# Weight conversions move their exponent word from SBUF to a PSUM bank, and GpSimd waits for earlier VectorE port work

## The chip, the cores and the metric

One core of one Trainium2 chip runs the whole program in one launch. The metric is device time in microseconds; lower is better. Engines are named as the profile names them: PE (TensorE matmul), DVE (VectorE), ACT (ScalarE), POOL (GpSimd), SP (SyncE, which issues most DMAs).

## The reference, cut to what matters

```
# 1. filter by FFT:   Y = rfft(x, axis=1) * (filt_r + 1j*filt_i);  y = irfft(Y)     x: 8 x 3072 x 256
# 2. top-1 experts over the 24576 rows of y: 8 experts, at most 768 tokens each
logits = x @ w_gate; e = argmax(logits); gate_w = softmax(logits)[e]
h = maximum(disp[e] @ w1[e], 0);  y = h @ w2[e]        # 256 -> 1024 -> 256; dropped tokens give 0
out[i] = gate_w[i] * y[...]
# 3. dense block on every row; w_in and w_out come as float64
h = x @ w_in                                            # 256 -> 2048
g = maximum(h, 0) + log1p(exp(-abs(h)))
return (g @ w_out).astype(float32)                      # 2048 -> 256
```

## The kernel before, in words

Tokens fill the experts in order, so the kernel filters the first three of the eight batches statically (STATIC = 3), and filters more only if a flag at the end says that an expert still has room. The expert part runs in 16 units of 384 tokens (UNIT), an expert and one half of its capacity each. Every float32 product is split into a high and a low part, so each matmul is done three times (high by high, high by low, low by high). The splits are made by ACT, which rounds to the high part (names in h: w1h, hh, gh, yh), and by POOL or DVE, which subtract to get the low part (w1l, w2l, gl on POOL; hl, yl, xl on DVE).

A unit transposes its tokens (pt), multiplies by w1 (pw, then hh and hl), by w2 (py, then yh and yl), by w_in (pi, then softplus in ACT's ab, ab, ln and DVE's g, then gh and gl) and by w_out (po). w_in and w_out are float64 in memory, and there are 16 conversions of 128x512 pieces: for each, `split_res` reads the two 32-bit words of a number. DVE first masks the mantissa into a scratch word v, combines it with the low word into wf, then overwrites v with the exponent field (three instructions); ACT scales the exponent word; DVE adds the sign to v and multiplies wf by it (two instructions); ACT and POOL split wf. In the planner these parts are the nodes ("c", n, 0) to ("c", n, 4). The scratch v is named pv where it lies in PSUM and wv where it lies in SBUF. Conversions 0 to 5 borrow v from the PSUM pool psy (3 banks, tag y), 6 to 8 from pso (2 banks), and 9 to 15 have it in SBUF (TURN = (6, 9)). psa is a third PSUM pool, of 3 banks.

Each batch also makes a table that sorts tokens to expert slots. The gate's DVE steps (nodes ("g", b, 4) and on; oh at L473, ctot at L496) and the one-hot tiles lo and hv (L512, eight pairs in each batch) belong to it; POOL multiplies hv by the token number, PE sums the table, DVE adds it up (ts).

The first part, about 310 us long, mixes all this: the three batches, the conversions and units 0 to 3. Its order is found by `Plan` as the program is built. Each piece of work is a node with an engine, a cost in ns, nodes that it comes after, and buffers of rings that it takes and gives (BUFS). A greedy list scheduler keeps a clock for each engine and picks the node that can start first; of equals the one whose chain of successors is longest, to which the table LIFT adds. Nodes with lock=True on DVE or POOL also share one clock named port: of those the scheduler lets one run at a time. The resulting list is written out in order, so every engine gets its instructions in the list's order and waits in it only for data and buffers. The scheduler's clock itself waits for nothing on the chip: nothing keeps a DVE and a POOL node with lock=True apart when the program runs. From step 16 on (STEPS), units follow in a fixed order by steps, in which each of the three products of a unit has its turn; there a unit's py takes two of psy's three banks.

Of the kernel before, what the change touches and what calls it, by code (L numbers as in the profile page):

```python
# [24 lines left out]
UNIT = 384  # L25
# [70 lines left out]
class Plan:  # L96
# [2 lines left out]

    BUFS = {"a": 3, "y": 3, "o": 2, "it": 4, "z": 3, "t2": 2, "j": 4, "yt": 3, "xt": 8, "s1": 3, "e0": 1, "e1": 1,  # L100
            "gx": 1, "gsb": 1, "lo": 2, "wst": 3, "wf": 2, "ws": 5, "w1h": 3, "w2h": 3, "xd": 3, "x": 2, "h": 4, "Y": 3,
            "wv": 1, "ln": 3, "g": 3, "gg": 4}
    LIFT = {"c_12": 45110, "c_15": 107406, "gl_0": 14316, "hh_3": 46195, "keep": 221952, "park_2": 380830,
            "t_0": 212010761652706638821731995831060079811112206336, "t_1": 416284, "t_2": 112004,
            "w2_1": 54516, "w2_2": 36883, "wi_0": 39454, "wo_0": 6694, "xh_3": 73006, "xl_1": 157432,
            "yh_0": 152114}
    MID = 4000
    HOP = {"PE": 250, "ACT": 130, "DVE": 130, "POOL": 100, "SP": 0}

# [92 lines left out]
def body(tc, cap, x, ff, fx, wg, w1, w2, win, wout, m1, m2, m3, m4, small, out):  # L202
# [14 lines left out]
    idxd = dram.tile([2, 128, nblk], I32, name="idxd")  # L217
    mid = [dram.tile([N1 * N2, D], F32, name=f"mid{b}") for b in range(1, STATIC)]
    psa = ctx.enter_context(tc.tile_pool(name="psa", bufs=3, space=PSUM))
    psy = ctx.enter_context(tc.tile_pool(name="psy", bufs=3, space=PSUM))  # L220
    pso = ctx.enter_context(tc.tile_pool(name="pso", bufs=2, space=PSUM))

    sm = const.tile([128, small.shape[1]], F32, name="sm")
    ident = sm[:, 0:128]
# [16 lines left out]
    ebias = const.tile([128, 1], F32, name="ebias")  # L241
    nc.vector.memset(ebias, -8.0 * 0x38000000)


    class Conv:

# [92 lines left out]
        def s2(self, b, kk):  # L339


            its = [self.it.pop((b, 2 * kk + f)) for f in range(2)]
            ps = [psy.tile([128, 2, D], F32, name="p3", tag="y") for _ in range(2)]
            for f in range(2):
                for c in range(4):
                    for a in range(2):
                        rows = slice(64 * a, 64 * a + 64)
                        nc.tensor.matmul(ps[a][32 * c:32 * c + 32, f],
                                         lhsT=self.m2s[rows, 4 * kk + 2 * f + c % 2, 32 * (c // 2):32 * (c // 2) + 32],
                                         rhs=its[f][rows, c % 2], start=True, stop=True)  # L350
            self.ps["s2", b, 2 * kk], self.ps["s2", b, 2 * kk + 1] = ps
# [206 lines left out]
        nc.vector.scalar_tensor_tensor(out=si, in0=slot, scalar=-1.0, in1=free, op0=ALU.add, op1=ALU.add)  # L558
        return gi, si

    class P:
        pass

    def wi_pools(st, tag):
        pool = lambda n, b: st.enter_context(tc.tile_pool(name=tag + n, bufs=b, side="right", reuse_waits="tile"))
        wp = pool("wi", 1)
# [33 lines left out]
    def split_res(q, which, space):  # L600
# [10 lines left out]
        if f64:  # L611
            two = t.bitcast(U32).rearrange("p (f two) -> p f two", two=2)
            lw, hw = two[:, :, 0], two[:, :, 1]
            if space is None:
                v = P.wl.tile([128, 512], U32, name="wv", tag="wv", bufs=1)
            else:
                v = space.tile([128, 512], U32, name="pv", tag="y" if space is psy else "o")
            f = P.wl.tile([128, 512], F32, name="wf", tag="wf")
            nc.vector.tensor_scalar(v, hw, 0xFFFFF, 0x100000, op0=ALU.bitwise_and, op1=ALU.bitwise_or)  # L619
            nc.vector.scalar_tensor_tensor(out=f, in0=lw, scalar=2.0 ** -32, in1=v, op0=ALU.mult, op1=ALU.add)  # L620
            nc.vector.tensor_scalar(v, hw, 0x7FF00000, None, op0=ALU.bitwise_and)  # L621
            yield 0
# [33 lines left out]
    class Unit:  # L656
# [211 lines left out]
    with tc.manual_schedule():  # L868
# [182 lines left out]
        def make_room():  # L1051
            stf.close()
            right_pools(stw, "M")

        def low_room():
            ste.close()
            low_pool(stw, "M")
# [27 lines left out]
            q = i % 4  # L1085
            return max(16 * (v - 2) + 4 * q - (8 if i < 4 else 6), -7 if i < 4 else -4)

        STEPS, HEAD, TURN = 16, 4, (6, 9)
        early = [(v, i) for v in range(2) for q in range(4) for i in (q, q + 4)] + [(2, i) for i in (0, 4, 1, 5)]
        pieces = early + [p[1:] for p in sorted((split_at(v, i), v, i) for v in range(2, len(units)) for i in range(8)  # L1090
                                                if (v, i) not in early)]
# [12 lines left out]
        for v in range(HEAD):  # L1104
# [12 lines left out]
            for j in range(8):  # L1117
# [7 lines left out]
                add(("hl", v, j), "DVE", 557, lambda u=u, j=j: u.w1_l(j), after=[("hh", v, j)], give=[("a", n)])  # L1125
                if v < 2 or 16 * (v - 2) + 2 * j < STEPS:
                    add(("w2", v, j), "PE", 1044, lambda u=u, j=j: u.w2_p(j),
                        after=[("hl", v, j), ("wl", v, 4 + j // 2)] + [],
                        behind=[("w2", v, j - 1)] if j else [("w2", v - 1, 7)] if v else [],
                        take=["y", "y"] if j == 0 else [],  # L1130
                        give=[("h", ("hh", v, j)), ("w2h", ("wh", v, 4 + j // 2))], tail=2000)
            for d in range(2 if ("w2", v, 7) in plan.node else 0):
                add(("yh", v, d), "ACT", 490, lambda u=u, d=d: u.y_h(d), after=[("w2", v, 7), "low"],
                    take=["Y"] if d == 0 else [], behind=[("yh", v, 0)] if d else [])
                add(("yl", v, d), "DVE", 550, lambda u=u, d=d: u.y_l(d), after=[("yh", v, d)],
                    give=[("y", ("w2", v, 0))])


        spaces, turn = [psy, pso, None], ["y", "o", "wv"]
        res = [(q, which) for which in range(2) for q in range(KI // 2)]  # L1140
        for n, (q, which) in enumerate(res):
            kind = (n >= TURN[0]) + (n >= TURN[1])
            load(("r", n), lambda q=q, which=which: load_res(q, which), 512, after=["x_done"], take=["wst"], behind=[("r", n - 1)] if n else [])
            stage = lambda: step_of(conv, n, lambda q=q, which=which, kind=kind: split_res(q, which, spaces[kind]))
            room = ["x_done", ("tf", last, 11)] if n < WI0 else ["room"] if n < KI // 2 else ["left"]
            add(("c", n, 0), "DVE", 1560 if kind == 2 else 2070, stage(), after=[("r", n), *room], take=[turn[kind], "wf"],
                behind=[("c", n - 1, 2)] if n else [], lock=kind == 2)
            add(("c", n, 1), "ACT", 663, stage(), after=[("c", n, 0)])
            add(("c", n, 2), "DVE", 1375, stage(), after=[("c", n, 1)], give=[(turn[kind], ("c", n, 0)), ("wst", ("r", n))])
# [7 lines left out]
        for v, u in enumerate(units):  # L1157
            for i in range(KI):
# [10 lines left out]
                if t + 4 < STEPS:  # L1169
# [2 lines left out]
                        behind=prior("wo", v, i - 1) if i else [("s4", last, 15), ("g", last, 10), "flags"] +  # L1172
                        [("c", n, 2) for n in range(*TURN)])

        order = plan.order(plan.LIFT)
        assert len(order) == len(plan.node)
        for n in order:
            plan.node[n][2]()


        at = {}
# [199 lines left out]
```

## Time and profile before

| | us |
|---|---|
| median of 3 runs | 1074.15 (1073.12 to 1076.38) |
| profiled execution, its own time | 1073.57 |
| its span, first to last instruction | 1071.7 |
| PE busy | 1029.2 |
| DVE, ACT, POOL busy | 495.9, 778.7, 600.5 |

The span is what the profile shows; the profiled execution's own time is 1.9 us more, which lies around it. Busy times are averages over two very different parts, the planned one up to about 310 us and the steps behind it, so the rows below take them apart by stretches of time.

### The profile page before, as it was taken

How to read it: one execution, taken by the hardware profiler on the slowest of the kernel's cores; microseconds unless marked ns; L12 is line 12 of the kernel's file. 1: busy time of each engine (PE TensorE's matmuls, PEld its weight loads, DVE VectorE, ACT ScalarE, POOL GpSimd, SP SyncE). 2: the span in 40 equal slices, each digit the busy share in tenths (PEclk: the TensorE clock that was granted, in tenths of full speed). 3: DMA queues.
4: the chain of work that ended last, by engine and by line, in shares of the span. 5: the costliest groups of instructions: out<-in, count | busy, mean ns of one | idle time of the engine just before them, and what ended most of it. 6: DMA issues, size and time to landing. Idle time of an engine off the chain costs nothing.

```text
span 1071.7 us, 19029 instructions
## 1 busy us (share of the span) xinstructions
PE 1029.2 (96%) x7112; PEld 954.9 (89%) x7112; DVE 495.9 (46%) x887; ACT 778.7 (73%) x1612; POOL 600.5 (56%) x560
## 2 busy tenths in 40 slices
PE   8999999898899999999999999999999999999994
PEld 7655666697899999999999999999999999999994
DVE  3856799899877433233323233333333233333221
ACT  4565568666677777777778777787877787878882
POOL 0513445587575556866666665657575747554553
PEclk9999999999899999999999999999999999999997
DMA  9978638553111453333332332322121212100000
GB/s 283 292 231 238 204 93 275 185 184 116 55 35 40 172 197 133 124 114 124 106 121 95 113 116 105 133 91 69 40 70 48 72 41 69 31 16 1 16 16 18
DMA packets 72822, 120.03 MB, mean 112 GB/s; under 512 B 6928, under 2 KB 46736, under 8 KB 72720
## 3 DMA queue, kind: packets, MB, share of 16 engines
q1 hardware_dynamic: 65424, 96.69, 28.1%
q0 software_dynamic: 4608, 12.59, 3.4%
q10 hardware_dynamic: 2688, 9.44, 2.7%
q8 instruction: 58, 0.95, 0.4%
q14 instruction: 44, 0.36, 0.1%
HBM read 71.51 MB, written 47.19 MB: 111 GB/s over the span
## 4 chain that ended last, share of the span: by engine, by line
PE 67%; DVE 4%; issue 2%; POOL 1%; ACT 1%; DMA 0%; POOLq 0%; DVEq 0%; ACTq 0%
PE po L816 23%; PE pi L784 23%; PE pw L730 10%; PE py L759 10%; POOL gl L801 1%; DVE wf L620 1%; PE pt L707 1%; DVE g L650 1%; DVE wv L619 0%; DVE wv L621 0%; DVE wf L627 0%; DVE hl L742 0%; DVE wv L625 0%; DMA out_dram<-ot,si 0%; ACT ab L643 0%
## 5 line engine op out<-in xcount | busy, mean ns | idle before, releaser
L650 DVE SCALAR_TENSOR_TENSOR g<-pi,ln 128x384 f32<-128x384 f32 x256 | 142.3, 556 | 478.6 <-ACT ln L645 418.6
L801 POOL TENSOR_TENSOR gl<-g,gh 128x384 fp32r<-128x384 f32 x256 | 260.4, 1022 | 125.7 <-ACT gh L796 122.0
L816 PE MATMUL po<-woh,gh 128*128 128x256 f32 x768 | 216.3, 282 | 3.8 <-DVE ot L823 3.8
L816 PE MATMUL po<-woh,gl 128*128 128x256 f32 x768 | 216.1, 281 | 0.0
L816 PE MATMUL po<-wol,gh 128*128 128x256 f32 x768 | 215.9, 281 | 0.0
L642 ACT ACTIVATE ab<-pi 128x384 f32<-128x384 f32 x256 | 124.5, 486 | 122.2 <-PE pi L784 116.0
L784 PE MATMUL pi<-yh,wih 128*128 128x384 f32 x512 | 173.2, 338 | 2.0 <-DVE g L650 2.0
L784 PE MATMUL pi<-yh,wil 128*128 128x384 f32 x512 | 173.5, 339 | 0.0
L784 PE MATMUL pi<-yl,wih 128*128 128x384 f32 x512 | 173.3, 338 | 0.0
L682 POOL TENSOR_TENSOR w1l<-ws,w1h 128x512 fp32r<-128x512 f32 x64 | 83.5, 1305 | 119.3 <-ACT w1h L677 91.8
L816 PEld LDWEIGHTS po<-woh,gh 128*128 128x128 f32 x768 | 144.0, 188 | 6.3 <-ACT ab L642 2.5
L816 PEld LDWEIGHTS po<-wol,gh 128*128 128x128 f32 x768 | 145.0, 189 | 0.0
L816 PEld LDWEIGHTS po<-woh,gl 128*128 128x128 f32 x768 | 144.7, 188 | 0.0
L645 ACT ACTIVATE ln<-ab 128x384 f32<-128x384 f32 (+1 forms) x257 | 134.9, 525 | 8.1
L643 ACT ACTIVATE ab<-ab 128x384 f32<-128x384 f32 (+1 forms) x257 | 134.8, 525 | 8.1
L796 ACT CAST gh<-g 128x384 fp32r<-128x384 f32 x256 | 129.8, 508 | 4.3 <-DVE g L650 3.6
L682 POOL TENSOR_TENSOR w2l<-ws,w2h 128x512 fp32r<-128x512 f32 x64 | 84.2, 1316 | 54.8 <-ACT w2h L677 54.8
L784 PEld LDWEIGHTS pi<-yh,wih 128*128 128x128 f32 x512 | 96.5, 188 | 2.6 <-DVE g L650 2.6
L784 PEld LDWEIGHTS pi<-yl,wih 128*128 128x128 f32 x512 | 96.5, 188 | 0.0
L784 PEld LDWEIGHTS pi<-yh,wil 128*128 128x128 f32 x512 | 96.4, 188 | 0.0
L730 PE MATMUL pw<-xh,w1h 128*128 128x384 f32 x256 | 88.3, 345 | 6.2 <-DVE g L650 3.4
L368 POOL TENSOR_TENSOR z<-z,t 128x512 f32<-128x512 f32 x36 | 46.5, 1293 | 77.6 <-DVE t L363 72.1
(146 smaller groups left out, 1932.3 us busy)
## 6 DMA issues: line engine op xcount, KB each, us to landing
ws<-in_w_dram SPq DMA_DIRECT2D x128, 256.0 KB, 2.9
out_dram<-cs SPq DMA_DIRECT2D x48, 512.0 KB, 4.0
xt<-in_x_dram SPq DMA_DIRECT2D x24, 384.0 KB, 7.5
mid<-s ACTq DMA_DIRECT2D x16, 384.0 KB, 4.5
rowsd<-yt SPq DMA_DIRECT2D x16, 384.0 KB, 3.7
it<-mid SPq DMA_DIRECT2D x24, 256.0 KB, 4.2
wst<-in_win_dram SPq DMA_DIRECT2D x8, 512.0 KB, 5.3
wst<-in_wout_dram SPq DMA_DIRECT2D x8, 512.0 KB, 3.7
```

Of the source, the lines that this page charges most:

```text
L368: nc.gpsimd.tensor_tensor(out=z, in0=z, in1=t2, op=ALU.add)
L642: nc.scalar.activation(out=ab[:, :n], in_=h, func=ACTF.Abs)
L643: nc.scalar.activation(out=ab[:, :n], in_=ab[:, :n], func=ACTF.Exp, scale=-1.0)
L645: nc.scalar.activation(out=ln[:, :n], in_=ab[:, :n], func=ACTF.Ln, bias=1.0)
L650: nc.vector.scalar_tensor_tensor(out=g[:, :n], in0=h, scalar=0.0, in1=ln[:, :n], op0=ALU.max, op1=ALU.add)
L682: nc.gpsimd.tensor_tensor(out=lo, in0=self.ws.pop(i), in1=hi.bitcast(F32), op=ALU.subtract)
L730: nc.tensor.matmul(ps, lhsT=a[:, k, fs], rhs=b[:, k], start=(n == 0), stop=(n == 5))
L759: nc.tensor.matmul(self.py[d], lhsT=a[:, j % 2, ds], rhs=b, start=(j == 0 and n == 0), stop=(j == 7 and n == 2))
L784: nc.tensor.matmul(pi, lhsT=a[i // 2][:, i % 2, k], rhs=b[:, k], start=(n == 0), stop=(n == 5))
L796: nc.scalar.copy(gh, self.g[i])
L801: nc.gpsimd.tensor_tensor(out=gl, in0=g, in1=gh.bitcast(F32), op=ALU.subtract)
L816: nc.tensor.matmul(self.po[t], lhsT=a[:, ts], rhs=b[:, i], skip_group_check=True, start=(i == 0 and n == 0 and t != 1), stop=(i == KI - 1 ...
```

## The change

It has four parts. **The bank.** The pools psa (3 banks) and pso (2) stay; psy is opened as P.py and lives until a node "turn", which closes it and opens two pools in its three banks: psw with 2 banks for py (ring yy) and psv with 1 bank for v (ring v). All of the conversions 6 to 15 take v from that bank; in the planner they are no longer lock=True. py is made in psw from the first unit on, so its first tile stands behind "turn". **The wait.** When the list is written out, the last instruction of each DVE node with lock=True is remembered, and the first instruction of every POOL node with lock=True that follows in the list gets a semaphore wait for it. There is no such wait the other way. **The order.** LIFT has other numbers, and with the other rings they give another list in the planned part. **The steps.** Their order stays; py alternates between two banks where it had three.

```diff
-            "wv": 1, "ln": 3, "g": 3, "gg": 4}
-    LIFT = {"c_12": 45110, "c_15": 107406, "gl_0": 14316, "hh_3": 46195, "keep": 221952, "park_2": 380830,
...
+            "yy": 2, "v": 1, "ln": 3, "g": 3, "gg": 4}
+    LIFT = {"c_10": 12614.0, "c_15": -10845.0, "hl_0": 91105.0, "hl_3": 34417.0, "keep": 221107.0,
...
-    psy = ctx.enter_context(tc.tile_pool(name="psy", bufs=3, space=PSUM))
     pso = ctx.enter_context(tc.tile_pool(name="pso", bufs=2, space=PSUM))
+    ctx.push(lambda *_: P.close.close())
...
+    def wide(name):
+        P.close = ExitStack()
+        P.py = P.close.enter_context(tc.tile_pool(name=name, bufs=3, space=PSUM))
+
+    wide("psy")
...
-                v = space.tile([128, 512], U32, name="pv", tag="y" if space is psy else "o")
+                pool, tag = space()
+                v = pool.tile([128, 512], U32, name="pv", tag=tag)
...
+        def turn():
+            P.close.close()
+            P.close = ExitStack()
+            P.py = P.close.enter_context(tc.tile_pool(name="psw", bufs=2, space=PSUM, reuse_waits="tile"))
+            P.pv = P.close.enter_context(tc.tile_pool(name="psv", bufs=1, space=PSUM, reuse_waits="tile"))
...
-        STEPS, HEAD, TURN = 16, 4, (6, 9)
+        STEPS, HEAD, TURN = 16, 4, (6, 6)
...
-                        after=[("hl", v, j), ("wl", v, 4 + j // 2)] + [],
+                        after=[("hl", v, j), ("wl", v, 4 + j // 2), "turn"],
...
-                        take=["y", "y"] if j == 0 else [],
+                        take=["yy", "yy"] if j == 0 else [],
...
-        spaces, turn = [psy, pso, None], ["y", "o", "wv"]
+        spaces = [lambda: (P.py, "y"), lambda: (pso, "o"), lambda: (P.pv, "v")]
+        add("turn", "SP", 0, turn, after=[("tf", last, k) for k in range(12)] + [("c", n, 2) for n in range(TURN[0])])
...
-            add(("c", n, 0), "DVE", 1560 if kind == 2 else 2070, stage(), after=[("r", n), *room], take=[turn[kind], "wf"],
-                behind=[("c", n - 1, 2)] if n else [], lock=kind == 2)
+            add(("c", n, 0), "DVE", 2070, stage(), after=[("r", n), *room] + ["turn"] * (kind > 1), take=[tag, "wf"],
+                behind=[("c", n - 1, 2)] if n else [])
...
+        lanes = {"DVE": mybir.EngineType.DVE, "POOL": mybir.EngineType.Pool}
         order = plan.order(plan.LIFT)
         assert len(order) == len(plan.node)
+        held = None
         for n in order:
+            here = len(nc.cur_bb.bb.instructions)
             plan.node[n][2]()
+            if plan.node[n][7] and len(nc.cur_bb.bb.instructions) > here:
+                new = [i for i in nc.cur_bb.bb.instructions[here:] if i.engine == lanes[plan.node[n][0]]]
+                if plan.node[n][0] == "DVE":
+                    held = new[-1]
+                elif held is not None:
+                    tc.add_manual_dep(new[0], held.name, mybir.DependencyInfo(
+                        mybir.DependencyClass.Sync, mybir.DependencyReason.DATA), reason="shared port")
```

The line numbers of the changed kernel are 7 to 27 higher; L512 of before is L521 there, L619 is L626, and so on.

Three places show what the change does to an engine's row. First DVE late in the planned part, before: the end of one conversion and the start of the next, with the scratch word in SBUF (wv), and the next softplus sum g behind them.

```order
L625 SCALAR_TENSOR_TENSOR wv<-wst,wv 128x512
L627 SCALAR_TENSOR_TENSOR wf<-wf,wv 128x512
L619 TENSOR_SCALAR wv<-wst 128x512
L620 SCALAR_TENSOR_TENSOR wf<-wst,wv 128x512
L621 TENSOR_SCALAR wv<-wst 128x512
L650 SCALAR_TENSOR_TENSOR g<-pi,ln 128x384
L742 SCALAR_TENSOR_TENSOR hl<-pw,hh 128x384
L512 TENSOR_TENSOR lo_82<-sm,ij_81 96x512
```

The same engine in the changed kernel, at the corresponding place.

```order
L632 SCALAR_TENSOR_TENSOR pv<-wst,pv 128x512
L634 SCALAR_TENSOR_TENSOR wf<-wf,pv 128x512
L626 TENSOR_SCALAR pv<-wst 128x512
L627 SCALAR_TENSOR_TENSOR wf<-wst,pv 128x512
L628 TENSOR_SCALAR pv<-wst 128x512
L541 TENSOR_TENSOR ts<-ts,p_3064 128x48
L776 TENSOR_TENSOR yl<-py,yh 128x384
L521 TENSOR_TENSOR lo_81<-sm,ij_78 96x512
```

The five instructions of a conversion are the same in number and kind; their scratch operand is now in PSUM.

Second, the last gate step of batch 2 (ctot to ij) on DVE before: it stands behind both halves of conversion 7 and most of the first products of units 0 and 1.

```order
L625 SCALAR_TENSOR_TENSOR pv<-wst,pv 128x512
L627 SCALAR_TENSOR_TENSOR wf<-wf,pv 128x512
L742 SCALAR_TENSOR_TENSOR hl<-pw,hh 128x384
L496 TENSOR_TENSOR ctot<-ctot,cn 96x8
L497 TENSOR_TENSOR eo<-eo,ixf 96x32
```

In the changed kernel it stands between the two halves of conversion 6.

```order
L628 TENSOR_SCALAR pv<-wst 128x512
L749 SCALAR_TENSOR_TENSOR hl<-pw,hh 128x384
L723 TENSOR_TENSOR xl<-pt,xh 128x384
L505 TENSOR_TENSOR ctot<-ctot,cn 96x8
L506 TENSOR_TENSOR eo<-eo,ixf 96x32
```

So the table of batch 2 can start earlier, ahead of conversion 7.

Third, POOL, with the semaphores that each instruction waits for, before: the low parts of conversions 1 and 2 (wil) and the gathers of unit 0's tokens (xd).

```order
L519 TENSOR_TENSOR hv_85<-hv_85,sm 96x192 [waits DVE_49,PE_49]
L638 TENSOR_TENSOR wil_1362<-wf,wih_1358 128x512 [waits Activation_49]
L638 TENSOR_TENSOR wil_1363<-wf,wih_1359 128x512 [waits Activation_49]
L697 DMA xd<-rowsd,gi_2361 128x256 [waits DMAHW2_49,DMAHW3_49,DMAHW1_49,DMAHW4_49,DMAHW0_49,DVE_49]
L697 DMA xd<-rowsd,gi_2361 128x256 x2
```

The same in the changed kernel.

```order
L528 TENSOR_TENSOR hv_82<-hv_82,sm 96x192 [waits PE_49]
L645 TENSOR_TENSOR wil_1314<-wf,wih_1310 128x512 [waits DVE_49,Activation_49]
L645 TENSOR_TENSOR wil_1315<-wf,wih_1311 128x512 [waits DVE_49,Activation_49]
L704 DMA xd<-rowsd,gi_2361 128x256 [waits DMAHW2_49,DMAHW3_49,DMAHW1_49,DMAHW4_49,DMAHW0_49,DVE_49]
L704 DMA xd<-rowsd,gi_2361 128x256 x2
```

Both wil now also wait for DVE: the first for the gate's oh of batch 2, the second for the end of batch 1's table.

## Rows read from the trace of the kernel before

**Rows 1.** Page, part 1: busy us of each engine (share, instructions).
```profile
PE 1029.2 (96%) x7112; PEld 954.9 (89%) x7112; DVE 495.9 (46%) x887; ACT 778.7 (73%) x1612; POOL 600.5 (56%) x560
```

**Rows 2.** Windows: stretch, length, busy us by engine, granted clock, DMA share, GB/s.
```profile
180.00:204.00 24.00, 20.68 (x101) 12.52 (x100) 20.94 (x45) 18.26 (x42) 11.08 (x12) 1.00 0.73 234
224.00:254.00 30.00, 23.36 (x132) 22.08 (x132) 27.38 (x46) 16.90 (x35) 22.31 (x20) 0.94 0.47 148
...
278.00:310.00 32.00, 27.15 (x172) 26.34 (x171) 28.45 (x41) 21.29 (x45) 18.23 (x17) 0.89 0.11 35
310.00:1000.00 690.00, 686.23 (x4556) 682.77 (x4556) 233.52 (x424) 535.34 (x1123) 423.17 (x396) 1.00 0.26 89
```

**Rows 3.** Waits of PE from 180 to 312 us: total us, times, longest.
```profile
PE pw L730 <- DVE g L650: 3.4, 1, 3.4
PE pt L707 <- DVE ts L532: 2.4, 1, 2.4
PE pw L730 <- DVE hl L742: 2.2, 1, 2.2
PE p L428 <- DVE j L393: 1.9, 1, 1.9
PE pt L707 <- DMA xd<-rowsd,gi: 1.9, 3, 0.8
```

**Rows 4.** Windows, instructions on the SBUF word wv alone: busy us (count).
```profile
150.00:312.00 162.00, 34.31 (x35) 5.05 (x7) 0.97 0.45 143
```

**Rows 5.** Windows, instructions on the PSUM word pv alone, same stretch.
```profile
150.00:312.00 162.00, 30.87 (x45) 5.96 (x9) 0.97 0.45 143
```

**Rows 6.** Groups by line and shape on DVE: xcount | busy us, mean ns.
```profile
L619 DVE TENSOR_SCALAR pv<-wst 128x512 uint32<-128x512 uint32 x9 | 6.2, 684 | 0.0
L619 DVE TENSOR_SCALAR wv<-wst 128x512 uint32<-128x512 uint32 x7 | 6.0, 864 | 0.0
...
L473 DVE TENSOR_TENSOR oh<-v,vm 96x256 f32<-96x256 f32 x3 | 4.4, 1480 | 0.0
...
L496 DVE TENSOR_TENSOR ctot<-ctot,cn 96x8 f32<-96x8 f32 x3 | 2.8, 928 | 0.0
```

**Rows 7.** Timeline of DVE: start us, duration us.
```profile
186.26 3.23 DVE L473 TENSOR_TENSOR oh<-v,vm 96x256 f32<-96x256 f32 x1
...
220.76 2.47 DVE L496 TENSOR_TENSOR ctot<-ctot,cn 96x8 f32<-96x8 f32 x1
...
243.92 6.03 DVE L512 TENSOR_TENSOR lo<-sm,ij 96x512 fp32r<-96x512 f32 x1
```

**Rows 8.** Tile lo from 180 to 312 us: duration ns min/median/max.
```profile
L512 DVE TENSOR_TENSOR lo<-sm,ij x10: 674/901/6034, 182.2 to 297.4; 96x512 fp32r<-96x512 f32 x10
```

**Rows 9.** Windows, DVE instructions on tile lo alone.
```profile
180.00:312.00 132.00, 16.40 (x10) 0.96 0.40 129
```

**Rows 10.** Timeline of POOL: start us, duration us.
```profile
186.54 2.49 POOL L638 TENSOR_TENSOR wil<-wf,wih 128x512 fp32r<-128x512 f32 x2
...
221.90 1.30 POOL L682 TENSOR_TENSOR w1l<-ws,w1h 128x512 fp32r<-128x512 f32 x1
...
243.50 1.28 POOL L682 TENSOR_TENSOR w1l<-ws,w1h 128x512 fp32r<-128x512 f32 x1
...
248.42 0.98 POOL L801 TENSOR_TENSOR gl<-g,gh 128x384 fp32r<-128x384 f32 x1
```

**Rows 11.** Timeline of PE at the two clocks: start us, duration us.
```profile
282.98 0.52 PE L730 MATMUL pw<-xl,w1h 128*128 128x384 f32 x1
...
289.56 0.34 PE L730 MATMUL pw<-xl,w1h 128*128 128x384 f32 x1
```

**Rows 12.** Timeline of DVE in the first batch: a table waits for PE.
```profile
72.27 0.69 DVE L512 TENSOR_TENSOR lo<-sm,ij 96x512 fp32r<-96x512 f32 x1 [2.41 <-PE p L527]
```

**Rows 13.** Timeline of the later stage: end of one unit, start of the next.
```profile
617.80 1.08 DVE L769 TENSOR_TENSOR yl<-py,yh 128x384 fp32r<-128x384 f32 x2
...
622.92 0.33 PE L759 MATMUL py<-hh,w2h 128*128 128x384 f32 x1
```

More of the change, by code (lines that the diff above doesn't have):

```diff
@@ L101 @@
             "gx": 1, "gsb": 1, "lo": 2, "wst": 3, "wf": 2, "ws": 5, "w1h": 3, "w2h": 3, "xd": 3, "x": 2, "h": 4, "Y": 3,
-            "wv": 1, "ln": 3, "g": 3, "gg": 4}
-    LIFT = {"c_12": 45110, "c_15": 107406, "gl_0": 14316, "hh_3": 46195, "keep": 221952, "park_2": 380830,
-            "t_0": 212010761652706638821731995831060079811112206336, "t_1": 416284, "t_2": 112004,
-            "w2_1": 54516, "w2_2": 36883, "wi_0": 39454, "wo_0": 6694, "xh_3": 73006, "xl_1": 157432,
-            "yh_0": 152114}
+            "yy": 2, "v": 1, "ln": 3, "g": 3, "gg": 4}
+    LIFT = {"c_10": 12614.0, "c_15": -10845.0, "hl_0": 91105.0, "hl_3": 34417.0, "keep": 221107.0,
+            "park_2": 374450.0, "su_0": 25618.0, "t_0": 5.2642809135285573e+51, "t_1": 406929.0,
+            "t_2": 44830.0, "turn": 125636.0, "xh_1": 100850.0, "xl_2": 103004.0, "yh_1": 27623.0,
+            "yl_2": 5645.0}
     MID = 4000
@@ L242, in body @@
     nc.vector.memset(ebias, -8.0 * 0x38000000)
+    class P:
+        pass
+    def wide(name):
+        P.close = ExitStack()
+        P.py = P.close.enter_context(tc.tile_pool(name=name, bufs=3, space=PSUM))
+    wide("psy")
     class Conv:
@@ L342, in s2 @@
             its = [self.it.pop((b, 2 * kk + f)) for f in range(2)]
-            ps = [psy.tile([128, 2, D], F32, name="p3", tag="y") for _ in range(2)]
+            ps = [P.py.tile([128, 2, D], F32, name="p3", tag="y") for _ in range(2)]
             for f in range(2):
@@ L559, in slot_index @@
         return gi, si
-    class P:
-        pass
     def wi_pools(st, tag):
@@ L752, in w2_p @@
             if j == 0:
-                self.py = [psy.tile([128, UNIT], F32, name="py", tag="y") for _ in range(2)]
+                self.py = [P.py.tile([128, UNIT], F32, name="py", tag="y") for _ in range(2)]
             hi, lo = self.wv[4 + j // 2]
@@ L1135, in body @@
                 add(("yl", v, d), "DVE", 550, lambda u=u, d=d: u.y_l(d), after=[("yh", v, d)],
-                    give=[("y", ("w2", v, 0))])
-        spaces, turn = [psy, pso, None], ["y", "o", "wv"]
+                    give=[("yy", ("w2", v, 0))])
+        spaces = [lambda: (P.py, "y"), lambda: (pso, "o"), lambda: (P.pv, "v")]
+        add("turn", "SP", 0, turn, after=[("tf", last, k) for k in range(12)] + [("c", n, 2) for n in range(TURN[0])])
         res = [(q, which) for which in range(2) for q in range(KI // 2)]
@@ L1142, in body @@
             kind = (n >= TURN[0]) + (n >= TURN[1])
+            tag = "yov"[kind]
             load(("r", n), lambda q=q, which=which: load_res(q, which), 512, after=["x_done"], take=["wst"], behind=[("r", n - 1)] if n else [])
@@ L1145, in body @@
             room = ["x_done", ("tf", last, 11)] if n < WI0 else ["room"] if n < KI // 2 else ["left"]
-            add(("c", n, 0), "DVE", 1560 if kind == 2 else 2070, stage(), after=[("r", n), *room], take=[turn[kind], "wf"],
-                behind=[("c", n - 1, 2)] if n else [], lock=kind == 2)
+            add(("c", n, 0), "DVE", 2070, stage(), after=[("r", n), *room] + ["turn"] * (kind > 1), take=[tag, "wf"],
+                behind=[("c", n - 1, 2)] if n else [])
             add(("c", n, 1), "ACT", 663, stage(), after=[("c", n, 0)])
-            add(("c", n, 2), "DVE", 1375, stage(), after=[("c", n, 1)], give=[(turn[kind], ("c", n, 0)), ("wst", ("r", n))])
+            add(("c", n, 2), "DVE", 1375, stage(), after=[("c", n, 1)], give=[(tag, ("c", n, 0)), ("wst", ("r", n))])
             add(("c", n, 3), "ACT", 615, stage(), after=[("c", n, 2)])
@@ L1233, in body @@
         stw.close()
+        P.close.close()
+        wide("psg")
     fv = nc.values_load(flag[0:1, 0:1], min_val=0, max_val=1)
```

## Prediction

> **What bounds the kernel now.** I read the page first. PE is busy in 96% of the span [rows 1], so only three things can make the kernel faster: less idle time on PE, fewer microseconds at a low clock, or a shorter tail. The windows say where they are [rows 2]. From 310 to 1000 us PE is busy for 686.23 of 690 us at full clock; nothing is to be had there. From 180 to 310 us it is different. In three stretches PE idles 24 - 20.68 = 3.3, 30 - 23.36 = 6.6 and 32 - 27.15 = 4.9 us, 14.8 in all, and two of them have a mean granted clock under 1 (0.94 and 0.89). The two levels are seen in single matmuls: the same one takes 0.52 us just after a long wait and 0.34 soon after [rows 11], which is 1.2 against 2.4 GHz. The loss in busy time is (1 - 0.94) x 23.36 = 1.4 and (1 - 0.89) x 27.15 = 3.0 us, 4.4 in all.
>
> Next, who is waited for. The longest waits of PE there all name DVE: for g 3.4, for ts 2.4, for hl 2.2, for j 1.9 us; the gathers (DMA xd) account for 1.9 [rows 3]. DVE is busy 20.94 of 24, 27.38 of 30 and 28.45 of 32 us in these stretches, more than any other engine but PE [rows 2]. So the planned part is bound by DVE in places, and what DVE does in vain there PE pays for. Of the 14.8 us of idle I take off the gathers' 1.9, which the change doesn't touch: 12.9 us of idle and 4.4 of low clock, **17.3 us, are what DVE's lateness costs**.
>
> Last, why DVE is late. Its instructions are stretched. The 35 on wv take 34.31 us, 4.90 for each of seven conversions [rows 4]; the 45 on pv take 30.87 us, 3.43 for each of nine [rows 5]. The difference, 1.47 x 7 = **10.3 us**, is time lost in conversions 9 to 15. The table's lo has a least duration of 674 ns and a greatest of 6034 [rows 8]; ten of them take 16.40 us [rows 9], 16.40 - 10 x 0.67 = 9.7 too much. The gate's oh at 186.26 takes 3.23 us [rows 7], where the three have 4.4 in all [rows 6], so that the other two have 0.59 each: 2.6 too much. ctot at 220.76 takes 2.47 of its group's 2.8, so 0.17 is its usual time: 2.3 too much. These locked nodes together lose **14.6 us**. What they stand against is seen in POOL: during lo's 6.03 us from 243.92 POOL runs one piece after another, from 243.50 to 249.40, five instructions in a row [rows 7, 10].
>
> **The change part by part.** *The bank.* Seven conversions (9 to 15) go from 4.90 to 3.43 us on DVE: 10.3 us less. I take the mean of pv, whose instructions keep one duration. Conversions 6 to 8 only change banks: nothing. Bounds: below, nothing gained, if pv beside POOL's denser work were stretched like wv; above, the 10.3.
>
> The SBUF form has one advantage: an undisturbed mask into wv is short. Its group's mean is 864 ns with the disturbed ones in it, against 684 for pv [rows 6], so the trace's mean speaks for PSUM. The Trainium skill (VectorE: DVE Perf Modes, "Why PSUM operands drop a tier") says that a PSUM operand keeps a float32 copy or scalar operation out of its faster two-port mode, which speaks against this change. By the page alone (an estimate: a mask at half of 684 ns before, so 14 x 0.34 = 4.8 us more) the bank would be a loss of 4.8 us on DVE; by the trace, whose sums contain both effects, it is a gain of 10.3. The same skill (SBUF — State Buffer, "Who interferes with whom") says that an instruction with at most one SBUF input outside that mode doesn't meet GpSimd, which would explain pv's constant duration; the trace agrees with 684 and 864 ns.
>
> *The wait.* It holds back only POOL work that stands behind the DVE node in the list. At oh both wil (2.49 us from 186.54 [rows 10]) would wait: the hv ahead of them ends at about 186.6, so oh would end at 187.2 instead of 189.5, 2.3 us earlier. At ctot only the w1l at 221.90 stands behind it: 1.3 of the 2.3. At the long lo four of the five POOL pieces stand ahead of it, and only the gl at 248.42 (0.98) would wait: 1.0 of 5.4. That is 4.6 of 10.3, 45%. The other lo's I take alike: of 14.6 us the wait removes 6.6 and leaves **8.0**, if POOL runs as late against DVE as now. Bounds: 0 and 14.6.
>
> What the wait costs: queued behind it in POOL's order are wil, w1l, w2l and gl, for which PE's conversions, first and second products and the output product wait. Behind the gate and table of batch 2 there are some 16 such waits. Each can hold POOL for the DVE node's own time, 0.67 us for a lo [rows 8], so at most 11 us. But POOL is idle 12.9, 7.7 and 13.8 us in the three stretches [rows 2], and among the long waits of PE [rows 3] none is for w1l, w2l or gl. I take nothing and keep the 11 us for a rival.
>
> *The later py and the two banks.* The first py stands behind "turn", so behind conversion 5; five first products stand ahead of it instead of three, so PE has work meanwhile. In the steps, a unit's last yl ends at 617.80 + 1.08 = 618.88, and the next unit's first py begins at 622.92 [rows 13]; two banks must be free there, and 4.0 us cover it. I take nothing. Without that cover each of 13 later units would lose what yl is late.
>
> *The order.* PE issues the same matmuls, the queues the same DMAs. The last gate step of batch 2 moves ahead of conversion 7, which lets its table begin earlier; I give it no time of its own, and 2.2 us (PE's wait for hl [rows 3]) would be the most.
>
> **The sum.** DVE's 10.3 + 14.6 = 24.9 lost microseconds cost PE 17.3: 0.69 for each. What stays, 8.0 us, goes on costing 0.69 x 8.0 = 5.5. So 17.3 - 5.5 = 11.8 us are gained, and the profiled execution's 1073.57 becomes 1061.8. The median lies 0.6 above that execution: **1062**.
>
> **The rivals.** *A, as summed* (58%): 1062, own range 1058 to 1066.
>
> *B, the bank works and the wait doesn't* (16%). POOL is late by its gathers and splits, so that what stands ahead of a locked DVE node is still running when DVE comes to it; the long lo is the model, where the wait would have removed 1.0 of 5.4. DVE then gains 10.3 x 0.69 = 7.1 us for PE: 1067. Against it: oh and ctot, of which it removes 3.6 of 4.9.
>
> *C, all of it goes* (12%): DVE is ahead of its work and PE finds everything in time, 17.3 us: 1057. For it: the three long waits are each fed by several stretched instructions in a row, and with shorter waits the clock need not fall either. A mechanism that would do it is that a stretched instruction loses only to the POOL instruction that is running, at most 1.3 us; the five in a row of [rows 10] speak against that. The Trainium skill (SBUF — State Buffer, "Who interferes with whom") has that rule, that whoever starts first holds the port for its whole instruction; the trace differs, since 6.03 us go over five instructions.
>
> *D, the wait closes a circle* (8%): slower. lo needs a buffer that PE's table product frees, and DVE waited 2.41 us for that in the first batch [rows 12]; POOL would now wait for lo, and PE for the gl and w1l behind it. If each of batch 2's eight tables put such a round on PE's path, 8 x 2.41 = 19.3 us come back: 1081. It takes five rounds (11.8 / 2.41) to lose the whole gain. Against it: POOL's idle time, and that the list puts each table product well ahead of the lo that needs its buffer.
>
> *E, nothing measurable* (6%): PE meets in the same stretch a next limit, ACT, which has 16.90 us of work in 30 and 21.29 in 32 [rows 2]. At the share that it reaches later, 535.34 of 690, 78%, its 38.2 us fit in 49 of these 62 us, so it would hold only a gain beyond 13 us; it needs ACT's order to be bad. 1073.
>
> **Numbers.** 0.3% of 1074 is 3.2 us, about what a measurement of this kernel can tell from no change. A, B and C are faster by more, 86%, less a little for their tails: 0.85. Same: 0.06. Slower: 0.09. The range goes from C's end, 1055, to beyond B, 1070; D and E stay outside.
>
> **What would show it.** In the changed kernel's trace the 50 DVE instructions on pv of conversions 6 to 15 should have a mean near 0.69 us, none above 0.8. lo's sum from 180 us on should fall from 16.40 to about 12, and oh to 0.6 to 0.8 us. PE should idle some 6 us less between 180 us and the end of the planned part, with at most one stretch at low clock, and hl and g should name DVE less often. For B, lo stays above 15 us. For D, PE's waits name POOL's w1l, w2l or gl, and POOL's name DVE's lo and hv. I am wrong if the steps beyond 310 us show new waits for yl, or if batch 2's zs on POOL, on which PE's next transform stage depends, comes later because it now waits for the gate of batch 1.

## The result and the profile after

The changed kernel takes **1055.87 us** (median of 4 runs, 1054.09 to 1057.97) beside 1074.07 for the kernel before on the same chip: ratio 0.9828, 95% interval 0.9804 to 0.9853, 18.2 us less. Its profiled execution took 1055.38 us with a span of 1053.5. The forecast of 1062 had the sign and the place; it put the gain 6 us too low.

The page, part 1, answers to [rows 1]: busy us, share and instructions.

```profile
PE 1025.5 (97%) x7112; PEld 954.0 (91%) x7112; DVE 472.8 (45%) x887; ACT 778.6 (74%) x1612; POOL 594.7 (56%) x560
```

Of the 18.2 us by which the span fell, PE's busy time gives 1029.2 - 1025.5 = 3.7 and its idle time the other 14.5. Less time at the low clock is part of the 3.7: reckoned as in the prediction, the low clock cost 4.4 us before and costs (1 - 0.90) x 21.84 + (1 - 0.95) x 19.31 = 3.2 in the windows below; for the other 2.5 these rows show no reason. VectorE is busy 23 us less for the same 887 instructions. The windows, to be held against [rows 2], say where:

```profile
180.00:204.00 24.00, 21.84 (x98) 14.63 (x97) 18.93 (x44) 17.50 (x40) 12.47 (x13) 0.90 0.76 247
204.00:224.00 20.00, 19.31 (x112) 18.68 (x111) 16.79 (x38) 12.71 (x25) 14.55 (x14) 0.95 0.49 149
224.00:254.00 30.00, 30.00 (x187) 29.95 (x186) 29.18 (x49) 26.17 (x53) 26.39 (x25) 1.00 0.58 182
278.00:310.00 32.00, 32.00 (x218) 31.86 (x218) 16.46 (x36) 25.64 (x55) 19.05 (x19) 1.00 0.10 30
310.00:1000.00 690.00, 686.32 (x4567) 682.95 (x4566) 229.90 (x418) 538.44 (x1129) 419.35 (x393) 1.00 0.26 87
```

In the second stretch of [rows 2] PE was busy 23.36 of 30 us, now all 30; in the third 27.15 of 32, now all 32. What is left lies at 195 to 210 us. From 310 to 1000 us PE is as busy as before. All waits of PE from 180 to 312 us, where [rows 3] had a list led by VectorE (total us, times, longest):

```profile
PE pt L714 <- DMA xd<-rowsd,gi: 1.9, 2, 1.4
PE py L766 <- DVE wf L634: 0.7, 1, 0.7
```

The conversion's five forms on VectorE, tile pv from 150 to 312 us (count, ns min/median/max), answer to [rows 4 to 6]:

```profile
L626 DVE TENSOR_SCALAR pv<-wst x16: 672/684/697, 153.1 to 275.0; 128x512 uint32<-128x512 uint32 x16
L627 DVE SCALAR_TENSOR_TENSOR wf<-wst,pv x16: 687/689/690, 153.9 to 275.8; 128x512 f32<-128x512 uint32 x16
L628 DVE TENSOR_SCALAR pv<-wst x16: 694/695/696, 154.6 to 276.5; 128x512 uint32<-128x512 uint32 x16
...
L632 DVE SCALAR_TENSOR_TENSOR pv<-wst,pv x16: 669/686/906, 156.6 to 281.8; 128x512 uint32<-128x512 uint32 x16
L634 DVE SCALAR_TENSOR_TENSOR wf<-wf,pv x16: 686/689/690, 157.3 to 282.5; 128x512 f32<-128x512 f32 x16
```

The windows, VectorE on tile lo alone, busy us and count, answer to [rows 9]:

```profile
180.00:312.00 132.00, 9.11 (x10) 0.97 0.43 136
```

Of the 80 instructions of the sixteen conversions all but one (0.906 us) keep one duration, and ten lo fell from 16.40 to 9.11 us.

### The profile page after: what moved, and what is told of

Same layout as the page of the kernel before. It is cut to its first block, busy times and chain, and to the rows that moved or that the text cites. A ratio compares the mean times of both kernels' runs of the same rounds, so it can differ in the third digit from the quotient of the medians.

```text
span 1053.5 us, 19028 instructions
## 1 busy us (share of the span) xinstructions
PE 1025.5 (97%) x7112; PEld 954.0 (91%) x7112; DVE 472.8 (45%) x887; ACT 778.6 (74%) x1612; POOL 594.7 (56%) x560
## 4 chain that ended last, share of the span: by engine, by line
PE 92%; POOL 2%; issue 2%; DVE 2%; ACT 1%; DMA 1%; POOLq 0%; DVEq 0%
PE pi L791 24%; PE po L823 24%; PE pw L737 13%; PE py L766 13%; PE p L437 3%; PE p L385 3%; PE p L332 2%; PE p L357 2%; PE p L398 2%; PE p L309 1%; POOL gl L808 1%; PE pt L714 1%; PE p L536 1%; PE pg L411 1%; DMA xd<-rowsd,gi 0%
## 5 line engine op out<-in xcount | busy, mean ns | idle before, releaser
L766 PE MATMUL py<-hh,w2h 128*128 128x384 f32 x256 | 88.3, 345 | 0.7 <-DVE wf L634 0.7
```

Of the source, the lines that this page charges most:

```text
L766: nc.tensor.matmul(self.py[d], lhsT=a[:, j % 2, ds], rhs=b, start=(j == 0 and n == 0), stop=(j == 7 and n == 2))
```

## The experiments

The change is three changes at once: the bank, the GpSimd waits, and another order of the list. The question is what each is worth, and why the sum came out larger than forecast. Theory: VectorE's lateness was the whole cost and the terms were mis-sized. Rivals: the order carries the gain; or bank and waits do the same thing twice.

### Taking parts out of the changed kernel

**e1_no_wait** leaves out the wait, in the list and on the bank of the change.

```diff
-                elif held is not None:
-                    tc.add_manual_dep(new[0], held.name, ...
```

> The changed kernel without the GpSimd waits: bank, list and everything else as in the changed kernel (1055.9 us). My sum: the wait frees VectorE of 4.6 to 7 us, so without it lo, oh and ctot are stretched again (lo's sum from 180 us above 13 us, changed kernel 9.1) and the time is 1059 to 1062. Rival B (bank and list do it, the wait nothing): 1055 to 1057, lo's sum about 9 to 10. Rival that the wait costs GpSimd time: below 1055.

**e3_sbuf** puts the word of conversions 6 to 15 back in SBUF, with list and waits unchanged; **e4_sbuf_no_wait** is this with e1's edit too.

```diff
-        spaces = [lambda: (P.py, "y"), lambda: (pso, "o"), lambda: (P.pv, "v")]
+        spaces = [lambda: (P.py, "y"), lambda: (pso, "o"), None]
```

> The changed kernel's list and waits, but conversions 6 to 15 keep the scratch word in SBUF (not locked, so GpSimd doesn't wait for them). If the bank is worth what I summed (1.47 us of VectorE time for each conversion, 0.69 of it on TensorE): ten conversions stretched to 4.9 us, 1064 to 1067. If the list alone keeps VectorE and GpSimd apart: conversions at about 3 us, 1055 to 1057. If the PSUM access costs more than the port: below 1055.

> The changed kernel's list alone: scratch word in SBUF and no GpSimd waits. If bank and wait make the gain: 1068 to 1074, near the kernel before. If the new list makes it: 1055 to 1060. If the effects add up, its distance from the changed kernel is the sum of those of the two runs that take away one.

Measured: e1 1062.13 us (ratio to before 0.9877, 0.9858 to 0.9896), e3 1075.23 (1.0010, 0.9996 to 1.0024), e4 1081.99 (1.0072, 1.0043 to 1.0101). In this list the waits are worth 6 to 7 us with or without the bank, and the bank 19 to 20. Without both, the list is slower than before. So e1 came out at the end of the range that was summed; e3 and e4 are slower than all of theirs, and a conversion with its word in SBUF takes 5.99 us in e3 and 5.71 in e4 where 4.9 was taken. The two effects add up: 19.4 + 6.3 = 25.7 us for the two runs that take one away, 26.1 for e4.

What a wait does is seen at one lo. First e1, VectorE and then GpSimd in the timeline (start, us):

```profile
226.81 7.31 DVE L521 TENSOR_TENSOR lo<-sm,ij 96x512 fp32r<-96x512 f32 x1
...
227.37 1.30 POOL L645 TENSOR_TENSOR wil<-wf,wih 128x512 fp32r<-128x512 f32 x1
228.62 1.30 POOL L689 TENSOR_TENSOR w1l<-ws,w1h 128x512 fp32r<-128x512 f32 x1
229.88 2.48 POOL L689 TENSOR_TENSOR w2l<-ws,w2h 128x512 fp32r<-128x512 f32 x2
232.32 1.25 POOL L689 TENSOR_TENSOR w1l<-ws,w1h 128x512 fp32r<-128x512 f32 x1
```

Then the changed kernel at the same place:

```profile
226.42 2.29 DVE L521 TENSOR_TENSOR lo<-sm,ij 96x512 fp32r<-96x512 f32 x1
...
226.87 1.28 POOL L645 TENSOR_TENSOR wil<-wf,wih 128x512 fp32r<-128x512 f32 x1
228.97 1.30 POOL L689 TENSOR_TENSOR w1l<-ws,w1h 128x512 fp32r<-128x512 f32 x1 [0.81 <-DVE lo L521]
```

In e1 GpSimd runs its pieces one behind the other (a sixth, a w2l, was already running when lo began), and lo ends at 234.12, 0.55 us behind the last of them. In the changed kernel GpSimd stands idle for 0.81 us before w1l, until lo is done, and lo loses only to what stands ahead of it in the list. TensorE's waits in e1 from 180 to 312 us show what hung on it:

```profile
PE pi L791 <- DVE hl L749: 4.6, 1, 4.6
PE p L437 <- DVE j L402: 1.9, 1, 1.9
PE pb L494 <- DVE cn L491: 1.3, 1, 1.3
PE pw L737 <- DVE hl L749: 0.9, 1, 0.9
```

They sum to 8.7 us, those of the changed kernel to 2.6; the difference, 6.1, is close to the 6.3 that the medians show. The 4.6 is the lo above: three hl stand behind it on VectorE.

### The wait alone, and the list numbers

**e2_wait_only** is the kernel before, with its own list and its SBUF word, plus the GpSimd waits. Since before's conversions 9 to 15 are marked as needing the port in their first half, GpSimd waits for these too.

```diff
+            if plan.node[n][7] and len(nc.cur_bb.bb.instructions) > here:
...
+                    tc.add_manual_dep(new[0], held.name, ...
```

> The kernel before with the GpSimd waits alone: its list, its LIFT and its SBUF scratch word, whose nodes are locked there, so that GpSimd also waits for the first half of conversions 9 to 15. If the wait is worth what I summed (45% of the locked nodes' 14.6 us): 1068 to 1071, and 6 of the list's waits show in oh (3.2 to under 1 us) and ctot. If it needs the new list, in which GpSimd work that stands ahead is not late: 1072 to 1075. If the circle of rival D exists it shows here: over 1077.

Measured: 1064.81 us, ratio 0.9924 (0.9899 to 0.9949): 8 to 10 us, below all three ranges and twice the forecast of its term. The long lo of [rows 7], on VectorE and then with GpSimd's pieces beside it (start, us):

```profile
244.64 2.65 DVE L512 TENSOR_TENSOR lo<-sm,ij 96x512 fp32r<-96x512 f32 x1
...
245.46 1.27 POOL L682 TENSOR_TENSOR w2l<-ws,w2h 128x512 fp32r<-128x512 f32 x1
247.51 1.29 POOL L682 TENSOR_TENSOR w2l<-ws,w2h 128x512 fp32r<-128x512 f32 x1 [0.79 <-DVE ts L532]
```

Of the five pieces that ran beside it before, the first two (w1l and w2l) run beside it still; the second w2l, and wol and gl after it, now start when lo is over (the profile names ts, which runs right behind lo). They stand behind lo in the list.

**e5_old_lift** gives the changed kernel before's table of list numbers; **e9_old_lift_no_wait** is the same without the waits.

```diff
-    LIFT = {"c_10": 12614.0, "c_15": -10845.0, "hl_0": 91105.0, ...
+    LIFT = {"c_12": 45110, "c_15": 107406, "gl_0": 14316, ...
```

> The changed kernel with the table of list numbers of before: PSUM bank and GpSimd waits, another list. Theory 1 (the prediction's terms hold in the old list, and the new list only packs the conversions more tightly): bank worth 7 and wait 5 to 10, so 1058 to 1063, conversions 3.45 us each, order nodes oh 0.6 us. Theory 2 (the bank is worth the 20 us seen at the new list in any list, the list numbers hardly matter): at or below the changed kernel, 1050 to 1056. Rival 3 (the list numbers carry the gain, the rest is small): 1064 or more.

> The kernel above without the GpSimd waits: the PSUM bank alone, with the table of list numbers of before. Theory 1 (the prediction's term of 7.1 us for the bank holds in the old list): 1066 to 1069 with lo summing to about 16 and oh 1.5 us each. Theory 2 (the bank is worth 20 us in any list): 1055 to 1058. Rival 3 (the bank is worth nothing without a list made for it): 1073 to 1076.

Measured: 1079.41 (1.0052, 1.0033 to 1.0070) and 1079.73 us (1.0049, 1.0030 to 1.0068). e5 lies in the range of its third rival, that the list numbers carry the gain; e9 lies in no range. The planner's nodes had changed with the bank, so the old numbers give neither the old order nor the new one but a third, and in it PE is busy only 14.74 of 24 us at 254 to 278. Its longest waits in e5 from 250 to 280 us:

```profile
PE p L536 <- DVE ts L541: 3.8, 1, 3.8
PE pi L791 <- DVE ts L541: 2.2, 1, 2.2
PE p L536 <- DVE g L657: 1.6, 1, 1.6
PE p L536 <- POOL hv L528: 1.4, 1, 1.4
```

So this pair says that the order alone can undo everything, and that in this order the waits are worth nothing (0.3 us); what the bank is worth it doesn't say. For that the order itself had to be held.

### Bank and waits in before's own order

**e10_before_order_bank** is the changed kernel with before's list written out, node by node, in place of the planner's, "turn" put in behind conversion 4, and no waits. The instructions on PE, VectorE, ScalarE, GpSimd and SyncE stand as in before; conversions 9 to 15 move from SBUF to the bank. Conversions 5 to 8 come to the same bank from other PSUM banks, and py has two banks as in the changed kernel; neither is taken apart from the bank here. **e11_before_order** has the waits too.

```diff
-        STEPS, HEAD, TURN = 16, 4, (6, 6)
+        STEPS, HEAD, TURN = 16, 4, (5, 5)
-        order = plan.order(plan.LIFT)
+        order = [named[w] for w in BEFORE.split()]
```

> Before's order of instructions on every engine, with the exponent word in PSUM for all 16 conversions (the pool reopened two plus one) and no GpSimd waits: the bank alone. Theory 1 (the prediction's term): 7 conversions of 4.90 fall to 3.43 us of DVE, times 0.69, 7.1 us less, 1067 to 1069. Theory 2 (the bank's 20 us come from the new list, which packs the conversions more tightly): 1070 to 1075. Theory 3 (the bank is worth 20 us in any list): 1053 to 1057.

> The kernel above with the GpSimd waits as well: bank and waits in before's order. Theory 1 (the prediction's bank and the 10 us that the waits alone measured add up): 1057 to 1060, with lo at 0.7 to 1.1 us each and no conversion op above 0.9 us. If the two overlap (each removes the same lateness of VectorE): 1061 to 1066. Theory 2 (bank worth nothing here): 1064 to 1065. Theory 3 (bank worth 20): 1045 to 1050.

**e12_order_alone** holds the other corner: the changed kernel's order, no waits, conversions 6 to 8 in the pool that before used, 9 to 15 in SBUF.

```diff
+            split_res(q, which, spaces[1 if 6 <= n < 9 else kind])     # spaces[2] is None
```

> The changed kernel's order of instructions alone: conversions 6 to 8 keep their word in the PSUM pool that before used for them, 9 to 15 in SBUF, and GpSimd doesn't wait. It parts the order's share of the 1082 us of the new list without bank and waits from that of its three further conversions in SBUF. If the order costs nothing by itself: 1073 to 1076, like before. If it is what costs: 1080 to 1084. From the three conversions taken at 5.71 less 3.43 us of VectorE and 0.69 to 0.79 of that in time: 4.7 to 5.4 us of the 1082 are theirs, so 1077. If the order gains without bank and waits what it gains with them (1060.3 less 1055.9): 1070.

Median us, and ratio to before (timed beside each) with its interval:

| | before's order | the new order |
|---|---|---|
| neither | 1074.07 (1) | e12 1077.40, 1.0021 (1.0011 to 1.0031) |
| waits | e2 1064.81, 0.9924 (0.9899 to 0.9949) | not run with seven words in SBUF; with ten, e3 1075.23 |
| bank | e10 1061.09, 0.9885 (0.9868 to 0.9901) | e1 1062.13, 0.9877 (0.9858 to 0.9896) |
| both | e11 1060.33, 0.9868 (0.9851 to 0.9884) | changed 1055.87, 0.9828 (0.9804 to 0.9853) |

In before's order the bank alone gives 13 us and the waits on top of it 0.8, which the intervals don't part from nothing. e10 lies between the ranges of its first and third theory, e11 between adding up and overlap; 13 and 9 alone and 14 together is overlap. In the new order the same waits give 6. The order by itself costs 2 us; with the bank it is worth nothing, with both 4.5, and as the intervals of the last two ratios just touch, that 4.5 is uncertain by some 3. Of e4's 1082, e12 gives 4.6 us to the three further conversions in SBUF, as expected of them.

Why the waits bring so little in before's order is read from the traces of e10 and e11. The two executions start unlike. GpSimd's first wait is for the first batch's gate, so none acts ahead of that gate's oh, which begins at 62.52 us in e10 and at 64.49 in e11 (PE waits 0.8 us for the input's DMA there and not in e10, and the rest has no named cause). So 2.0 us are taken off e11's times here. The timeline of e10, VectorE, GpSimd and PE (start, us, idle before):

```profile
62.52 0.60 DVE L482 TENSOR_TENSOR oh<-v,vm 96x256 f32<-96x256 f32 x1
...
193.25 1.20 POOL L704 DMA_INDIRECT xd<-rowsd,gi  x1 [4.11 <-DVE free L566]
194.04 1.93 PE L437 MATMUL p<-j,m4s 96*96 96x512 f32 x4 [1.92 <-DVE j L402]
199.98 0.33 PE L714 MATMUL pt<-sm,xd 128*128 128x128 f32 x1 [0.65 <-DVE pv L632]
```

The timeline of e11, the same pieces, and a matmul behind PE's long wait:

```profile
64.49 0.60 DVE L482 TENSOR_TENSOR oh<-v,vm 96x256 f32<-96x256 f32 x1
...
193.44 1.20 POOL L704 DMA_INDIRECT xd<-rowsd,gi  x1 [1.08 <-DVE free L566]
201.73 0.48 PE L714 MATMUL pt<-sm,xd 128*128 128x128 f32 x1 [2.74 <-DMA xd<-rowsd,gi]
205.37 0.52 PE L737 MATMUL pw<-xl,w1h 128*128 128x384 f32 x1
```

With the waits batch 2's oh takes 0.6 instead of 3.3 us, the gathers are issued 1.8 us earlier (193.44 - 2.0 beside 193.25), and PE has no wait for j. But the last of the three pieces of rows is transposed only 0.2 us earlier (201.73 - 2.0 beside 199.98): PE waits 2.74 us for it, and some ten matmuls behind this wait run at the lower level. What is won at j is lost at the rows. In the new order it is much the same up to there: the gathers go out 1.7 us earlier with the waits (189.91 beside 192.70, oh of the first batch at 62.10 beside 63.16), and PE then waits 1.9 us for rows. What the waits bring beyond that in the new order is the lo of 7.31 us and the 4.6 us that PE waits behind it. In before's order the bank alone has left no such lo, as e10's ten show (ns min/median/max):

```profile
L521 DVE TENSOR_TENSOR lo<-sm,ij x10: 678/1122/1905, 182.3 to 285.3; 96x512 fp32r<-96x512 f32 x10
```

### Can waiting do what the bank does?

**e8_sbuf_wait_conv** is e3 with conversions 6 to 15 counted among the nodes that GpSimd waits for.

```diff
+            conv_v = isinstance(n, tuple) and n[0] == "c" and n[1] >= TURN[1] and n[2] in (0, 2)
+            if (plan.node[n][7] or conv_v) and len(...
```

> The changed kernel's list with the exponent word of conversions 6 to 15 in SBUF, where the GpSimd nodes now wait for both VectorE parts of these conversions as they do for lo: can waiting do what the bank does? If yes: conversions near 3.5 us instead of 6.0, 1057 to 1063. If GpSimd then pays (its nodes are late, and what waits for gl, w1l and hv): conversions 4 to 5 us and 1065 to 1075. If the waits reach too few of the meetings: 1075, as without them.

Measured: 1072.49 us (0.9984, 0.9973 to 0.9995), in the second range. The windows of e3, the word in SBUF alone, VectorE's busy us for fifty instructions:

```profile
150.00:312.00 162.00, 59.90 (x50) 0.98 0.45 141
```

The same of e8:

```profile
150.00:312.00 162.00, 50.72 (x50) 0.96 0.45 143
```

Waiting takes 9.2 us of VectorE's time off ten conversions, from 5.99 to 5.07 each; the bank takes 25 (3.45). And lo pays: its ten rise from 8.65 to 13.2 us, as GpSimd, held at the conversions, meets them instead, and PE waits 4.1 us for GpSimd's hv, w1l and gl, for which it doesn't wait in e3. These waits can't replace the bank.

### What is left: the gathers

The changed kernel's PE waits 1.9 us for gathered rows, and behind it 18 matmuls are issued 0.32 us apart instead of 0.17, the clock's lower level: 2.7 us more. PE's last wait for rows, one slow matmul and one behind the slow stretch, in the changed kernel's timeline:

```profile
197.55 0.33 PE L714 MATMUL pt<-sm,xd 128*128 128x128 f32 x1 [1.45 <-DMA xd<-rowsd,gi]
...
200.31 0.52 PE L737 MATMUL pw<-xl,w1h 128*128 128x384 f32 x1
...
206.21 0.34 PE L737 MATMUL pw<-xh,w1l 128*128 128x384 f32 x1
```

**e6_swap** moves one group of step 4 into the pause; **e7_fill** fills the pause with repeats of the first tile's transposition, which is useless work.

```diff
+        order.remove(("pt", 0, 0))
+        order.insert(order.index(("s4", last, 15)) + 1, ("pt", 0, 0))
```

```diff
+                for _ in range((0, 6, 18)[t] if first else 0):
+                    nc.tensor.transpose(pt[:, 0:128], self.xd[0][:, k * 128:(k + 1) * 128], ident)
```

> The changed kernel with the first transposition of the first unit put behind the last matmul of step 4 in TensorE's order, so that one group of 0.86 us stands in the 1.9 us that TensorE waits for the gathered rows. If only idle time counts: 0.9 us less, 1055. If the shorter pause also spares the stretch at 1.2 GHz behind it (18 matmuls of 0.32 instead of 0.17 us apart, some 2.7 us): 1052 to 1053. If the rows land later with nothing won (the pause moves): 1055.9, no change.

> The changed kernel with 6 and 18 repeats of the first tile's transposition between the first, second and third of the first unit: useless work of about 2 us in the 0.44 and 1.45 us that TensorE waits for gathered rows. If the pause is what drops the clock: granted clock near 1.00 in 198 to 206, the matmuls there 0.33 us, 2.5 us less, 1053 to 1054. If the clock falls for another reason: the stretch at 1.2 GHz stays and the time is 1056 to 1057.

Measured: e6 1054.67 us (0.9816, 0.9801 to 0.9831), e7 1055.19 (0.9821, 0.9807 to 0.9836); neither differs from the changed kernel by more than the intervals, and e7 lies between its two ranges. The windows of e7 show the clock held:

```profile
180.00:204.00 24.00, 23.59 (x128) 15.86 (x127) 19.18 (x47) 18.40 (x42) 11.75 (x13) 1.00 0.77 240
204.00:224.00 20.00, 18.37 (x111) 17.73 (x111) 17.17 (x40) 12.73 (x25) 16.16 (x15) 1.00 0.53 165
```

The 2.7 us aren't gained in full, for PE, now earlier, meets the next wait. In e7 it has only this one from 180 to 312 us:

```profile
PE pw L740 <- DVE hl L752: 1.6, 1, 1.6
```

The waits of PE in e6, same stretch:

```profile
PE pb L494 <- DVE cn L491: 1.2, 1, 1.2
PE pw L737 <- DVE hl L749: 1.0, 1, 1.0
PE p L437 <- ACT pv L630: 0.7, 1, 0.7
PE pt L714 <- DMA xd<-rowsd,gi: 0.3, 1, 0.3
```

The slow matmuls had covered a wait for VectorE. These executions start unlike too (the first batch's oh at 62.10 us in the changed kernel, 63.55 in e6, 63.67 in e7); with that taken off, VectorE's work at 325 us comes 2.6 us earlier in e6 and 1.4 in e7. e6 is the best median, by 1.2 us, which is too little to call it faster.

## Why the prediction was right in kind and short in size

**What bounds the kernel: right.** VectorE's lateness was put at 17.3 us, 12.9 of idle time and 4.4 of low clock. The idle part is gone: the waits of PE for VectorE, four of the five [rows 3], are down to one of 0.7 us, and PE's idle time from 180 to 310 us (the windows' lengths less its busy time) from 15.95 to 2.85. The gathers' 1.9, left out of the 17.3, stays. Of the low clock some 3 us stay, now behind the wait for the gathers.

**The bank: VectorE's part right, its price in time too small.** Forecast 10.3 us of VectorE and 7.1 of time. In before's order the 80 conversion instructions fell from 34.31 + 30.87 = 65.2 [rows 4, 5] to 55.0 us, 10.2; but the time fell by 13.0. The term had left out that the conversions' end moves everything behind them: without any GpSimd wait ten lo fell from 16.40 to 11.54 us, the long one from 6.03 to 1.61, as they met GpSimd's pieces at other times. 15.1 us of VectorE gave 13.0 of time, 0.86 for each, not 0.69. In the new order the bank is worth 15.3 (e12 to e1).

**The wait: its size depends on what it is added to.** The term was 6.6 of VectorE's 14.6 lost us and 4.5 of time. It measured 8 to 10 alone, 0.8 on the bank in before's order, 6.3 in the new one. In e2, where the wait is alone, oh (0.59 us) and ctot (1.20) came out about as summed, and the long lo at 2.65 us where the sum had left 5.0: two of GpSimd's five pieces stand ahead of it in the list, not four. So the ten lo lose 4.1 us there, ctot 1.0 and oh nothing: 9.5 of the 14.6 are gone, 65% and not 45%. That misread row of pieces is the step that failed in this term; "if POOL runs as late against DVE as now" held there. That a wait stops lo only from losing to pieces behind it in the list was right, as this lo and the one of 2.29 us show. What the sum could not see is that the same wait is worth 0.8 or 6.3 us by what PE meets next.

**"I take nothing" for what GpSimd's waits cost: right for the change.** From 180 to 312 us PE waits for GpSimd neither in the changed kernel nor in e11. Where GpSimd is made to wait for the conversions as well, in e8, it costs 4.1 us of such waits.

**The order: the step that failed.** It was given "no time of its own", and 2.2 us at the most. Bank and waits in before's order give 1060.3, against a forecast that summed them to 1062: two mis-sized terms (13.0 and 0.8 for 7.1 and 4.5) made nearly the right sum, by luck. The other 4.5 of the 6 us (give or take 3) are the order's. The windows place them: PE is busy 58.29 of 60 us from 120 to 180 in e11 and 59.44 in the changed kernel (up to 180 us it waits 2.6 us for z in e11 and 1.4 in the changed kernel), 27.12 and 30.00 of 30 from 224 to 254 (it waits 1.8 and 1.1 us for hl there), 4.0 together. Which of the moved nodes does it was not tested. That the order costs 2 us without the bank and waits shows that it is one that fits them, not a better one by itself.

**Later py and two banks: right.** One py waits 0.7 us for conversion 5, and beyond 310 us no wait for yl appears.

**Rivals.** The time is C's 1057, and its condition held, PE finds VectorE's work in time; though not because a stretched instruction loses to one GpSimd piece only: e1's 7.31 us lo ran beside six. B's 1067, the bank without the wait, is e10 and e1, at 1061 to 1062. D's round was not seen in the changed kernel: no wait of PE names w1l, w2l or gl. Of the signs, pv's mean was as forecast with one instruction above 0.8 (0.906), oh 0.6, lo 9.1 for 12, and 13 us less idle for 6; one stretch of low clock is left before 310 us, at 200 to 206. Batch 2's last z on POOL begins at 153.39 us beside 154.72, so that sign of being wrong did not come either.

## What to carry to other kernels

Price each part of a change against the order in which it will run: bank and waits that were worth 13 and 9 us alone were worth 14 together in the old order and 21.5 in the new one (e12 to the changed kernel). Count in the list, not only in the timeline, which pieces a wait will hold. Before two traces are set side by side, look where each starts: here up to 2.4 us apart before the change could act. Numbers that steer a planner belong to the structure for which they were found; put on another they cost 23.5 us (e5 beside the changed kernel). And before a low clock or a wait is counted as gain, look what stands next: filling the pause here held the clock and uncovered a wait of 1.6 us.

## What the runs showed of the hardware

Here a VectorE operation with two SBUF operands loses not to one GpSimd instruction but to the whole row of them: in e1 7.31 us for a lo of 0.68, until 0.55 us behind the row's end; in the kernel before 6.03 us, again 0.55 behind; in the changed kernel 2.29, 0.56 behind the one piece left. And the mask into SBUF has a faster form than the mask into PSUM: in e12 the seven masks of L626 and L628 (ns, min/median/max) show it.

```profile
L626 DVE TENSOR_SCALAR wv<-wst x7: 410/424/1124, 242.4 to 294.9; 128x512 uint32<-128x512 uint32 x7
...
L628 DVE TENSOR_SCALAR wv<-wst x7: 427/1400/1459, 245.2 to 297.1; 128x512 uint32<-128x512 uint32 x7
```

The shortest takes 0.41 us, in PSUM 0.68. The Trainium skill (VectorE: DVE Perf Modes, "Why PSUM operands drop a tier") says that a PSUM operand keeps an operation out of the two-port mode; the trace agrees with 0.41 and 0.68 us. But the median of the second mask is 1.40 us (those that begin while GpSimd has a piece running take 1.37 to 1.46, those that don't 0.43), and over seven conversions SBUF cost 38.78 / 7 = 5.54 us each against 3.45. The rule was right and the other effect larger.
